# LSH attention and a spatial-gating feed-forward: query heads handled in pairs, on row and column tiles of TensorE

## The chip, the cores and the metric

The kernel runs on one core of a Trainium2 chip. A core has five engines that run their own instruction streams and meet at semaphores: TensorE (PE, matmuls, with its weight loads listed apart as PEld), VectorE (DVE), ScalarE (ACT), GpSimd (POOL) and SyncE (SP), which here only issues DMAs. Matmuls write PSUM; everything else lives in SBUF or in HBM. Sixteen DMA engines move data between HBM and SBUF and inside SBUF, and also transpose 16-bit tiles on the way. The metric is the device time of one execution in microseconds (us), the median of several runs.

## The reference

Inputs are q, k, v of shape 4 batches x 8 heads x 768 tokens x 64, a 64 x 6 hash projection, and the weights of one gated feed-forward. Everything is computed to float32 accuracy.

```python
q_bits = (einsum('bhsd,dk->bhsk', q, proj) > 0); k_bits = (einsum('bhsd,dk->bhsk', k, proj) > 0)
mask = q_bucket[:, :, :, None] == k_bucket[:, :, None, :]      # same 6-bit hash
scores = where(mask, (1 / sqrt(64)) * q @ k.T, -1e9)
scores = scores - max(scores, axis=-1)
attn = exp(scores); attn = attn / (sum(attn, axis=-1) + 1e-9)
x = (attn @ v)                    # heads side by side: batch x 768 x 512
h = maximum(x @ w_in, 0); u, g = h[..., :512], h[..., 512:]
g = (g - mean(g)) / sqrt(var(g) + 1e-6)                        # over the 512
out = (u * (w_spatial @ g + b_spatial[:, None])) @ w_out
```

A query row that matches no key has all scores at -1e9, so its softmax is uniform and its result is the mean of v. The weights w_in and w_out come as float64.

## The kernel before

**Accuracy.** Each float32 operand of a product is carried as two float16 parts, hi and lo, of the operand times a power of two. A product is three float16 products (hi hi, hi lo, lo hi) summed in float32 in PSUM.

**Attention, per head n and block i.** A head has six blocks of 128 rows. There are 32 heads (`N`) in 16 pairs; the two heads of a pair share one load of q and k (`load_qk`), one hash (`hash_rows`), one split (`split_qk`), with head 0 on partitions 0 to 63 and head 1 on 64 to 127. `build` then copies, by DMA, a head's parts into a buffer `ab` of four slots, so that one contraction over 128 rows does two of the three products (q lo with k hi stacked on q hi with k lo), and a second one does q hi with k hi and, on rows 64 to 75, the hash: rows of plus and minus 16384 and 32768 whose products cancel for equal bits and push a score down by multiples of 2^29 for unequal ones.

`scores` makes 128 query rows x 768 keys in two banks of PSUM (four matmuls of 384 columns), takes the row maximum by a VectorE pass whose main output `jk` is thrown away (L287), the exp on ScalarE with that maximum as bias (L289), a float16 hi part by a ScalarE cast (L292), the lo part by a subtraction on VectorE or GpSimd (L293), and a DMA transpose of both parts from `pp` into `pt` (L295), issued from SP's queue. `weighted` sums over keys with the transposed probabilities as stationary operand and v as moving operand, 65 columns wide: the 65th column of ones makes the softmax's sum. `normalize` divides by it, replaces rows without any match by the mean of v (`mean_v`), and writes hi and lo parts of x; `transpose_x` transposes these by DMA for the feed-forward.

Heads 1 to 8 (`KEYS`) go another way, that avoids the transposes: `row_max` computes all hi hi scores once more to get the maxima ahead, writes these as one more row of `ab`, and `scores_k` makes the scores with keys on partitions, so that exp needs no bias and `weighted_k` no transpose.

**Feed-forward, per batch.** `mlp_units` makes 28 units: six v units (x times the second half of w_in, then the normalisation), and per half of the tokens four u units, four s units (spatial product) and three o units (output). In each of these a group of 12 or 18 matmuls fills one bank of PSUM, and ScalarE, VectorE and GpSimd work on its result. The units of a batch are queued when its last head is normalised and then spread over the steps of the next batch by a credit counter. The last batch's units run at the end.

**Order of work.** The program is written as a loop over steps g, one per head and block. Each piece is given a priority by `at(step, k)`, smaller first; a planner simulates the engines and orders each engine's instructions by readiness and priority, one at a time, and semaphores are derived from that order. Engines execute their order strictly. `tc.issue_after(st["tr"])` keeps a DMA behind the latest transpose in SP's queue. Buffers are counted by `bufs`: PSUM has two score tiles of two banks (`ps_sc`), two banks for weighted sums (`ps_pv`) and two for everything else (`ps_m`); in SBUF there are three `ex`, three `pp`, five `pt`. The weights are loaded, converted and split in 37 pieces (`weights_gen`), spread by `W_AT` over the first steps.

Of the kernel before, what the change touches and what calls it, by code (L numbers as in the profile page):

```python
# [10 lines left out]
BF16 = mybir.dt.bfloat16  # L11
# [4 lines left out]
ALU = mybir.AluOpType  # L16
AX = mybir.AxisListType
ET = mybir.EngineType
# [3 lines left out]
NB = 6           # hash bits  # L22
EPS_LN = 1e-6

# Every float32 operand of a product is carried as hi + lo, two float16 parts of
# the operand times a power of two; three products (hh, hl, lh) are summed in
# float32 PSUM.
SQ = 32.0        # q, k, v
SX = 64.0        # x, w_in, gated, w_out
SN = 256.0       # v_n  # L30
SW = 4096.0      # w_spatial
HQ = 16384.0     # hash rows, q side
HK = 32768.0     # hash rows, k side (their product is the mask's penalty)
# [3 lines left out]
def lsh_attention_spatial_gating(  # L37
    ctx: ExitStack,
    tc: tile.TileContext,
    kq: bass.AP,      # [B, NPAIR, 128 = (head, d), (k, q), S]  # L40
    v: bass.AP,       # [B, NPAIR, 128 = p, (c, head), d], token = c * 128 + p
    hconst: bass.AP,  # [128, 34]: proj's columns for each hash row, what a row subtracts, its factor
    w_in: bass.AP,    # [512, 1024]
    w_sp: bass.AP,    # [s, t]
    b_sp: bass.AP,    # [768]
    w_out: bass.AP,   # [512, 512]
    out: bass.AP,     # [B, S, 512]
# [24 lines left out]
    nc.scalar.preload_act_table_set("natural_log_exp_and_others")  # L72
    ident = const.tile([P, P], F16, name="ident")
    make_identity(nc, ident)
    ones = const.tile([P, P], F32, name="ones")
    nc.gpsimd.memset(ones, 1.0)
# [3 lines left out]
    # operands of the scores, per head: slot 0 = q [lo; hi], 1 = k [hi; lo],  # L80
    # 2 = k hi + hash rows + a constant row, 3 = q hi + hash rows + the row of -max
    NAB = 4
    NR = D + 2 * NB
    ab = [const.tile([P, 4, S], F16, name=f"ab{i}") for i in range(NAB)]
    for i, t in enumerate(ab):
        eng = nc.vector if i % 2 else nc.gpsimd
        eng.memset(t[D:P, 2:4, :], 0.0)
        eng.memset(t[96:P, 2, :], HK)
    vp = [const.tile([P, 2 * NT, 130], F16, name=f"vp{i}") for i in range(2)]
    for t in vp:  # L90
        nc.gpsimd.memset(t[:, :, 2 * D:130], 1.0)

# [62 lines left out]
    def load(p):  # L155
        load_qk(p)
        load_v(p)
# [447 lines left out]
```

## Time and profile before

| what | before |
|---|---|
| timed runs, median (3) | 740.17 us (738.73 to 740.52) |
| profiled execution, first to last instruction | span 734.0 us |
| between that span and the timed median | 6.1 us |
| busy, PE / DVE / ACT / POOL | 609.5 / 558.3 / 463.8 / 374.8 us |
| mean granted TensorE clock | 0.940 |
| DMA transposes pt<-pp | 144 |
| operand copies ab<-hl | 65 |

The page names no other time of the profiled execution than its span; the time around it is taken as the difference to the median. In rows of groups, "L293 DVE ... x112 | 118.3, 1057" means line 293, VectorE, 112 instructions, 118.3 us busy in all and 1057 ns listed for one. Instructions on one engine can overlap at their edges, so busy times are less than count times mean, and PE's ends are modelled. In rows of stretches the engines stand in the order PE, PEld, DVE, ACT, POOL, followed by the granted clock (1.00 is full), the DMA share and GB/s. In rows of the time line the first number is the start and the second the length, both in us. In rows of one line, three numbers give the shortest, median and longest in ns. SPq and ACTq are the instruction queues that issue DMAs.

### The profile page before, as it was taken

The numbers are of one execution on the slowest core, as the hardware profiler recorded it, in microseconds if no ns is written. First come the engines' busy times: TensorE is split into PE (matmuls) and PEld (weight loads), VectorE is DVE, ScalarE is ACT, GpSimd is POOL, SyncE is SP. The second block draws the span as 40 slices with busy tenths as digits, with TensorE's granted clock in tenths as the row PEclk, the third lists the DMA queues.
The fourth block names the chain that finished last, engine by engine and source line by source line (L and its number), as shares of the span: only waits on it lengthen the run. The fifth ranks groups of instructions, "written<-read, shape, count | busy, mean of one in ns | idle before, by whom it ended". The sixth has DMA issues, their size and how long they took to land.

```text
span 734.0 us, 15600 instructions
## 1 busy us (share of the span) xinstructions
PE 609.5 (83%) x6024; PEld 365.5 (50%) x6024; DVE 558.3 (76%) x1012; ACT 463.8 (63%) x713; POOL 374.8 (51%) x353
## 2 busy tenths in 40 slices
PE   1686576786796986889898899989998998999997
PEld 0253343444554553555455555555455655654553
DVE  3879989998788899778589888789698876745100
ACT  1565476667878766866677767667677666743221
POOL 4236666669847577457315473436235562541503
PEclk9778888799999898999999999999999999999999
DMA  6783424233299988999999999999999999850011
GB/s 197 177 184 106 122 81 137 77 99 77 57 219 229 226 191 155 237 222 183 231 212 205 188 207 194 221 208 203 220 207 180 205 159 219 171 134 14 1 43 44
DMA packets 274842, 118.24 MB, mean 161 GB/s; under 512 B 255184, under 2 KB 258256, under 8 KB 274768
## 3 DMA queue, kind: packets, MB, share of 16 engines
q1 hardware_dynamic: 272464, 116.36, 76.3%
q10 hardware_dynamic: 2304, 0.89, 0.5%
q8 instruction: 47, 0.77, 0.4%
q14 instruction: 27, 0.22, 0.1%
HBM read 27.94 MB, written 6.29 MB: 47 GB/s over the span
## 4 chain that ended last, share of the span: by engine, by line
PE 33%; DMA 26%; DVE 18%; POOL 7%; issue 7%; ACT 6%; SPq 2%; ACTq 0%; DVEq 0%; POOLq 0%
DMA pt<-pp 21%; PE ups L396 6%; PE ops L426 6%; PE vps L355 5%; PE sps L411 4%; DVE jk L287 2%; DVE mh L229 2%; PE sp L285 2%; DMA ab<-hl 2%; PE sp L286 2%; ACT pp L292 2%; ACT ex L289 2%; PE pv L308 2%; DVE w L137 2%; DVE pp L256 1%
## 5 line engine op out<-in xcount | busy, mean ns | idle before, releaser
L289 ACT ACTIVATE ex<-sp,nb 128x768 f32<-128x768 f32 x144 | 129.1, 898 | 41.5 <-DVE jk L287 35.2
L292 ACT CAST pp<-ex 128x768 f16<-128x768 f32 x144 | 119.1, 829 | 54.9 <-DMA pt<-pp 49.3
L293 DVE TENSOR_TENSOR pp<-ex,pp 128x768 f16<-128x768 f32 x112 | 118.3, 1057 | 42.0 <-ACT pp L292 40.5
L287 DVE TENSOR_SCALAR_CACHE_REDUCE jk<-sp 128x768 bf16<-128x768 f32 x144 | 136.5, 948 | 16.4 <-PE sp L286 12.4
L308 PE MATMUL pv<-vp,pt 128*128 128x65 f16 x864 | 103.4, 197 | 25.7 <-DMA pt<-pp 25.1
L285 PE MATMUL sp<-ab 128*128 128x384 f16 x288 | 96.9, 337 | 32.9 <-ACT ex L289 24.7
L308 PEld LDWEIGHTS <-pt 128*128 128x128 f16 x864 | 82.9, 100 | 49.2 <-DMA pt<-pp 38.8
L310 PE MATMUL pv<-vp,pt 128*128 128x65 f16 x864 | 103.8, 198 | 0.0
L309 PE MATMUL pv<-vp,pt 128*128 128x64 f16 x864 | 103.5, 196 | 0.0
L411 PE MATMUL sps<-ws,vn 128*128 128x384 f16 x576 | 100.3, 327 | 0.0
L286 PE MATMUL sp<-ab 127*128 127x384 f16 x288 | 98.0, 341 | 0.0
L293 POOL TENSOR_TENSOR pp<-ex,pp 128x768 f16<-128x768 f32 x32 | 54.2, 1694 | 82.4 <-ACT pp L292 72.3
L309 PEld LDWEIGHTS <-pt 128*128 128x128 f16 x864 | 82.9, 100 | 11.9 <-issue 1.7
L310 PEld LDWEIGHTS <-pt 128*128 128x128 f16 x864 | 82.9, 100 | 3.4 <-issue 0.6
L396 PE MATMUL ups<-xt,wi 128*128 128x384 f16 x384 | 71.6, 342 | 0.7 <-DVE sg L168 0.7
L411 PEld LDWEIGHTS <-vn 128*128 128x128 f16 x576 | 54.8, 98 | 35.0 <-issue 1.1
L256 POOL TENSOR_TENSOR pp<-ex,pp 128x768 f16<-128x768 f32 x32 | 56.8, 1778 | 30.2 <-ACT pp L255 28.3
L426 PE MATMUL ops<-wo,g 128*128 128x512 f16 x288 | 68.4, 382 | 3.0 <-ACT wo L139 1.1
L355 PE MATMUL vps<-wi,xt 128*128 128x512 f16 x288 | 67.0, 382 | 0.0
L327 POOL TENSOR_TENSOR x<-x,xf 128x384 f32<-128x384 f32 x32 | 37.5, 1171 | 50.7 <-DVE x L326 43.0
L229 DVE TENSOR_REDUCE mh<-mp 128x1 f32<-128x384 f32 x96 | 50.6, 549 | 10.6 <-PE mp L227 9.8
L416 POOL TENSOR_TENSOR sy<-sy,u 128x384 f32<-128x384 f32 x32 | 36.0, 1124 | 44.0 <-DVE sy L415 43.5
(93 smaller groups left out, 1281.4 us busy)
## 6 DMA issues: line engine op xcount, KB each, us to landing
qk<-kq SPq DMA_DIRECT2D x16, 768.0 KB
ab<-hl SPq DMA_DIRECT2D x31, 384.0 KB
ab<-hl SPq DMA_DIRECT2D x34, 192.0 KB
v<-v SPq DMA_DIRECT2D x16, 384.0 KB
out<-o SPq DMA_DIRECT2D x24, 256.0 KB
raw<-w_in SPq DMA_DIRECT2D x16, 256.0 KB
pt<-pp SPq DMA_TRANSPOSE x144
raw<-w_sp SPq DMA_DIRECT2D x12, 192.0 KB
```

Source lines behind the costliest of these rows:

```text
L285: nc.tensor.matmul(ps[:, c], lhsT=t[:, 0, qs], rhs=t[:, 1, cs], start=True, stop=False)
L286: nc.tensor.matmul(ps[:, c], lhsT=t[0:P - 1, 3, qs], rhs=t[0:P - 1, 2, cs], start=False, stop=True)
L287: nc.vector.tensor_scalar(jk, ps, -ISQ, None, op0=ALU.mult, op1=ALU.min, accum_out=nb)
L289: st["ex", n, i] = nc.scalar.activation(ex, ps, AF.Exp, bias=nb, scale=ISQ).ins
L292: nc.scalar.copy(pp[:, 0], ex)
L293: (nc.gpsimd if i in (PL_POOL if n >= 2 * NH else PL_POOL1) else nc.vector).tensor_tensor(out=pp[:, 1], in0=ex, in1=pp[:, 0], op=ALU.subtract)
L308: nc.tensor.matmul(acc, lhsT=pt[:, c, :], rhs=vh, start=(i == 0 and c == 0), stop=False)
L309: nc.tensor.matmul(acc[:, 0:D], lhsT=pt[:, c, :], rhs=vl, start=False, stop=False)
L310: nc.tensor.matmul(acc, lhsT=pt[:, NT + c, :], rhs=vh, start=False, stop=(i == NT - 1 and c == NT - 1))
L396: nc.tensor.matmul(ps[:, :HS], lhsT=wi[gw][:, c, d * P:(d + 1) * P], rhs=xt[c][:, gx, hs], start=(k == 0), stop=(k == 3 * NPAIR - 1))
L411: nc.tensor.matmul(ps[:, :HS], lhsT=vn[gv][:, c, d * P:(d + 1) * P], rhs=ws[gw][:, c, hs], start=(k == 0), stop=(k == 3 * NT - 1))
L426: nc.tensor.matmul(ps, lhsT=gt[h][gg][:, c, j * P:(j + 1) * P], rhs=wo[gw][:, c, :], start=(k == 0), stop=(k == 3 * NF - 1))
```

## The change

The step becomes one pair of heads and one block of 128 queries: 96 steps of two heads each, all on one path. `ab`, `build`, `mean_v`, `row_max`, `scores_k`, `weighted_k`, `normalize` and `transpose_x` are gone, and so are the DMA issues from ScalarE's queue.

- Scores read the split q and k where they lie. Head 0's operands are on partitions 0 to 63, head 1's on 64 to 127; each product is a contraction over 64 rows at `tile_position` (0, 0) or (64, 0) of the array. Four such products per head and half of the keys (lo hi, hi lo, hi hi, and one for the hash rows, which lie in their own buffers `hr`), so 16 matmuls of 384 columns a step, the heads alternating.
- The hash rows are scaled on GpSimd (before: VectorE) and copied to `hr` by eight DMAs per pair from SP's queue.
- The maximum pass clips the scores at -2^27 and writes them to `ex` in SBUF; a row without any match is then flat and needs no special case. GpSimd negates and scales the two maxima, ScalarE takes the exp in place and sums it, GpSimd and a VectorE reciprocal turn the sums into factors, and the cast and the low part apply the factor. So the probabilities are normalised before they are cast. All low parts are on VectorE.
- The transposes write three blocks side by side (`pt` holds half of the queries). `weighted` then takes v as stationary operand, 64 columns for each head at `tile_position` (0, 0) or (0, 64), and the transposed probabilities as moving operand, 384 columns; the result is x already transposed, with both heads below each other, and its two parts are written by one ScalarE and one VectorE operation.
- Steps, buffers and due points follow: 96 steps, `LAG` 2, four `ex`, three `pp`, four (larger) `pt`, two `hl`, and half the values in `W_PTS`.

```diff
+    NHR = 3
+    NR = 2 * NB
+    hr = [const.tile([P, 2, S], F16, name=f"hr{i}") for i in range(NHR)]
...
-        nc.vector.tensor_scalar(s1, s0, hv[:, 1:2], None, op0=ALU.mult)
-        st["sg", p] = s1
+        nc.gpsimd.tensor_scalar(s1, s0, hv[:, 1:2], None, op0=ALU.mult)
+        for e in range(2):
+            for j in range(4):
+                nc.sync.dma_start(
+                    out=hr[p % NHR][D * e:D * e + NR, 1 - j // 2, (j % 2) * HS:(j % 2 + 1) * HS],
+                    in_=s1[32 * j + 16 * e:32 * j + 16 * e + NR, :])
...
+    def scores(p, i):
+        hl, hs = st["hl", p], hr[p % NHR]
+        qs = slice(i * P, (i + 1) * P)
+        ps = [ps_sc.tile([P, 2, 512], F32, tag="sc", name=f"sp{p}_{i}_{e}")[:, :, :HS] for e in range(2)]
         for c in range(2):
             cs = slice(c * HS, (c + 1) * HS)
+            for k, (a, b) in enumerate(((QL, KH), (QH, KL), (QH, KH), (None, None))):
+                for e in range(2):
+                    r = slice(D * e, D * e + D)
+                    lhsT, rhs = (hs[r, 1, qs], hs[r, 0, cs]) if a is None else (hl[r, a, qs], hl[r, b, cs])
+                    nc.tensor.matmul(ps[e][:, c], lhsT=lhsT, rhs=rhs, start=(k == 0), stop=(k == 3), tile_position=(D * e, 0))
...
+        for e in range(2):
+            nc.vector.tensor_scalar(ex[e], ps[e], -float(2 ** 27), None, op0=ALU.max, op1=ALU.max, accum_out=mx[:, e:e + 1])
+        nc.gpsimd.tensor_scalar(nb, mx, -ISQ, None, op0=ALU.mult)
+        for e in range(2):
+            nc.scalar.activation(ex[e], ex[e], AF.Exp, bias=nb[:, e:e + 1], scale=ISQ, accum_out=sm[:, e:e + 1])
+        nc.gpsimd.tensor_scalar(ri, sm, 1e-9, 1.0 / SP, op0=ALU.add, op1=ALU.mult)
+        nc.vector.reciprocal(ri, ri)
+        at(NT * p + i + G_H, 50)
+        h, j = divmod(i, NT // 2)
+        for e in range(2):
+            if j == 0:
+                st["pt", p, h, e] = wk.tile([P, 2 * NT, NT // 2, P], F16, tag="pt", bufs=PTB, name=f"pt{p}_{h}_{e}")
+            pp = wk.tile([P, 2, 2, HS], F16, tag="pp", bufs=PB, name=f"pp{p}_{i}_{e}")
+            nc.scalar.activation(pp[:, 0], ex[e], AF.Copy, scale=ri[:, e:e + 1])
+            nc.vector.scalar_tensor_tensor(out=pp[:, 1], in0=ex[e], scalar=ri[:, e:e + 1], in1=pp[:, 0], op0=ALU.mult, op1=ALU.subtract)
+            st["tr"] = nc.sync.dma_start_transpose(out=st["pt", p, h, e][:, :, j, :], in_=pp.rearrange("p g c k -> p (g c k)")).ins
+
+    def weighted(p, h):
+        vp = st["vp", p]
+        pt = [st.pop(("pt", p, h, e)) for e in range(2)]
+        ps = ps_pv.tile([P, 512], F32, tag="pv", name=f"pv{p}_{h}")[:, :HS]
         for c in range(NT):
+            for k, (gv, gp) in enumerate(((1, 0), (0, 0), (1, 1))):
+                for e in range(2):
+                    nc.tensor.matmul(ps[D * e:D * e + D], lhsT=vp[:, 2 * c + e, gv * D:gv * D + D],
+                                     rhs=pt[e][:, gp * NT + c], start=(c == 0 and k == 0),
+                                     stop=(c == NT - 1 and k == 2), tile_position=(0, D * e))
...
+        x = st["xt", p][:, :, h * HS:(h + 1) * HS]
+        f = SX / (SP * SQ)
+        nc.scalar.activation(x[:, 0], ps, AF.Copy, scale=f)
+        nc.vector.scalar_tensor_tensor(out=x[:, 1], in0=ps, scalar=f, in1=x[:, 0], op0=ALU.mult, op1=ALU.subtract)
...
+    for g in range(NP * NT + LAG + 1):
+        p, i = divmod(g, NT)
+        if p < NP:
+            at(g, 0)
+            scores(p, i)
+            at(g + 1, 300)
+            with tc.issue_after(st["tr"]):
+                if g == 0:
+                    split_v(0)
+                if i == 1 and p + 1 < NP:
+                    hash_rows(p + 1)
+                if i == 2 and p + 1 < NP:
+                    split_qk(p + 1)
...
+        while wv < 2 * NP and 3 * wv + 2 + LAG <= g:
+            m, h = divmod(wv, 2)
+            wv += 1
+            at(g, 200)
+            weighted(m, h)
+            if h == 1 and m % NPAIR == NPAIR - 1:
+                queue += mlp_units(m // NPAIR)
```

284 lines of the change are left out of this document (33 added, 251 removed).

## The prediction

> **What bounds the kernel now.** I read the page first, then the groups by line, then busy time by stretches, then the time line of a few microseconds, and last the chain of waits. A "unit" below is one head's 128 query rows against 768 keys; there are 192, two to a step of the changed kernel, so 96 steps.
>
> ```profile
> span 734.0 us, 15600 instructions
> PE 609.5 (83%) x6024; PEld 365.5 (50%) x6024; DVE 558.3 (76%) x1012; ACT 463.8 (63%) x713; POOL 374.8 (51%) x353
> ```
>
> No engine is full over the span. By stretches, with the busy time of PE, PEld, DVE, ACT, POOL, the granted clock, the DMA share and GB/s:
>
> ```profile
> 20.00:200.00 180.00, 124.57 (x1351) 75.56 (x1350) 159.47 (x287) 119.24 (x191) 112.57 (x103) 0.85 0.44 113
> 200.00:300.00 100.00, 82.79 (x790) 49.33 (x788) 91.84 (x168) 74.69 (x129) 64.08 (x59) 0.90 1.02 202
> 300.00:640.00 340.00, 308.06 (x3284) 190.54 (x3283) 272.26 (x495) 237.90 (x341) 156.59 (x145) 0.98 1.06 205
> ```
>
> and the exps of the third stretch, by line:
>
> ```profile
> L289 ACT ACTIVATE ex<-sp,nb x107: 883/900/923, 299.6 to 638.8; 128x768 f32<-128x768 f32 x107
> ```
>
> Up to 300 us VectorE is the fullest (159/180 = 0.89, then 0.92). From 300 to 640 TensorE is (308/340 = 0.91), while the DMA engines are full. That stretch holds 107 units, 6.36 us per two. The last 75 us are the last batch's feed-forward on TensorE (its rows come below). So DVE early, PE late, and a PE tail must be priced; a DMA saving counts only through waits in the third stretch.
>
> **VectorE, per step.**
>
> ```profile
> 27.25 0.08 DVE L287 DVE_READ_ACCUMULATOR jk<-sp 128x1 f32 x1
> 27.25 0.95 DVE L293 TENSOR_TENSOR pp<-ex,pp 128x768 f16<-128x768 f32 x1
> 28.12 0.95 DVE L287 TENSOR_SCALAR_CACHE_REDUCE jk<-sp 128x768 bf16<-128x768 f32 x1
> ```
>
> ```profile
> L323 DVE RECIPROCAL rv<-rv 128x6 f32<-128x6 f32 x32 | 5.9, 185 | 0.5
> ```
>
> Starts are 0.87 us apart, though each pass is listed with 0.95, and the read of the accumulator starts with the next pass: 0.87 is the price of a 768-wide pass in a full queue. The change gives every unit one max pass and one low-part pass, all on VectorE, and every step one reciprocal: 4 x 0.87 + 0.19 = 3.7 us. The max pass now writes float32 to SBUF; the accumulating pass above wrote bf16, and with float32 in and out from PSUM a plain pass is no dearer (below, L415: 551 ns for 384). I keep 0.87; the upper end is 1.06, the mean listed for L293 on VectorE beside a busy POOL (next fence), which would add 4 x 0.19 x 96 = 73 us of VectorE time. I stay low because POOL loses its 64 low parts and all of normalize.
>
> ```profile
> L293 DVE TENSOR_TENSOR pp<-ex,pp 128x768 f16<-128x768 f32 x112 | 118.3, 1057 | 42.0 <-ACT pp L292 40.5 <-POOL x L327 0.6 <-issue 0.2
> ...
> L177 DVE SCALAR_TENSOR_TENSOR hl<-qk,hl 128x768 f16<-128x768 f32 x16 | 19.2, 1203 | 9.0 <-ACT hl L176 8.7
> ...
> L415 DVE SCALAR_TENSOR_TENSOR sy<-sps,bt 128x384 f32<-128x384 f32 x32 | 17.6, 551 | 40.8 <-PE sps L411 40.6
> L205 DVE SCALAR_TENSOR_TENSOR vp<-v,vp 128x768 f16<-128x768 f32 x16 | 17.5, 1092 | 1.6 <-ACT vp L204 1.6
> L137 DVE SCALAR_TENSOR_TENSOR w<-raw,w 128x256 uint32<-128x256 uint32 x24 | 16.7, 694 | 0.1
> ```
>
> Kept beside it: the splits (two q/k passes of 19.2 become one of double width, v's is 17.5) plus 32 new x low parts at L415's 0.55 (17.6), with the hash thresholds some 80 us or 0.85 a step; four weight passes, the longest 16.7, some 60 us over the first 37 steps, 1.6 each; the feed-forward's L415, bn_stats and the scaling pass, which I take for 60 to 70, 0.7 a step from step 24. That makes 6.15 us for steps 0 to 23, 6.9 for 24 to 36, 5.3 after. Gone are the row-max reductions, normalize and one hash pass. In all 355 + 215 = 570: **VectorE is not relieved**, it only changes its work.
>
> **TensorE, per step.** Starts of matmuls tell the pace, not their listed length.
>
> ```profile
> 501.35 0.33 PE L286 MATMUL sp<-ab 127*128 127x384 f16 x1
> 501.51 0.19 PE L308 MATMUL pv<-vp,pt 128*128 128x65 f16 x1
> 501.54 0.19 PE L309 MATMUL pv<-vp,pt 128*128 128x64 f16 x1
> ```
>
> ```profile
> 659.09 15.54 PE vps L355 x72
> ...
> 728.12 2.39 issue
> ```
>
> From the start of the 384-wide matmul to the next is 0.16 (I use 0.165), from a 65-wide one 0.03. Two units now take 8 x 0.165 + 36 x 0.03 = 2.4 us. After, scores are 16 matmuls of 384 (K = 64, two row tiles), and the weighted sum 36 of 384 per three steps (M = 64, two column tiles): 2.64 + 1.98 = 4.6 us if nothing overlaps, 1.32 + 1.0 = 2.3 if every pair does. So **the tiling, if it works, buys back what it spends**; the saving is 96 row-max matmuls, 16 us, and the v means. Feed-forward stays at 69 us a batch (659.09 to 728.12), 2.9 a step from step 24; hashes add 0.23.
>
> ```profile
> 108.78 0.25 PE L270 MATMUL pv<-vp,pp 128*128 128x65 f16 x1
> 108.95 1.51 PE L163 MATMUL hp<-qk,hc 128*32 128x384 f32 x8
> ```
>
> ```profile
> L163 PE MATMUL hp<-qk,hc x4: 817/849/849, 5.6 to 5.7; 128*32 128x384 f32 x4
> ```
>
> Column tiles do overlap here: the hash's first four start within 0.1 us and each runs 0.82 to 0.85. I take 1.0 for the weighted sum. Row tiles are in no trace. Bounds are 1.32 and 2.64; I take **1.65**, nearer the paired end by the hash row, but not on it: head 0's PSUM tile is freed one pass (0.88) before head 1's, and matmuls are placed singly as they become ready, so part of head 0's run without a partner. The time line shows that habit, a single feed-forward matmul amid pv's:
>
> ```profile
> 508.36 0.19 PE L310 MATMUL pv<-vp,pt 128*128 128x65 f16 x1
> 508.40 0.38 PE L426 MATMUL ops<-wo,g 128*128 128x512 f16 x1
> ```
>
> Going from pv to the hash's tiles took 0.17 between starts where 0.06 was usual: 0.1 a switch, three a step, 0.3 (bounds 0 and, by a whole 0.33 matmul each, 1.0). Late steps: 1.65 + 1.0 + 2.9 + 0.23 + 0.3 = 6.1.
>
> The Trainium skill (TensorEngine Tiling (Array Packing), Key Properties) says that changing the tiling mode drains the array. The hash row agrees that a switch costs something; if a drain were the 0.33 - 0.165 left of one matmul, an estimate, three would be 0.5 and 72 late steps 14 us longer.
>
> **What lies beside.**
>
> ```profile
> L292 ACT CAST pp<-ex 128x768 f16<-128x768 f32 x144 | 119.1, 829 | 54.9 <-DMA pt<-pp 49.3 <-issue 2.2 <-ACT ex L289 1.4
> ```
>
> ```profile
> L318 POOL TENSOR_SCALAR fl<-nb x32: 225/232/1009, 36.2 to 644.0; 128x6 f32<-128x6 f32 x32
> ```
>
> ScalarE has two exps (0.90 in the row of the third stretch) and two casts (0.83) a step, the casts now with a scale per row (0.83 to 0.90, as the exp with its bias), and two sums read out, an operation no row shows: 0 to 0.2, I take VectorE's 0.08. That is 3.7, and with splits, weights and feed-forward (it was busy 463.8, of which exps and casts of 192 units are some 330) about 5.1, under the others; it also sheds 96 DMA issues. POOL's two small operations a step (0.23 each, 1.0 when something is ahead) sit in the chain max, negate, exp, reciprocal, cast; two steps of exp buffers hide them, and without that cover a step would be 7 us of pure chain.
>
> ```profile
> ab<-hl SPq DMA_DIRECT2D x31, 384.0 KB
> ab<-hl SPq DMA_DIRECT2D x34, 192.0 KB
> ```
>
> ```profile
> L295 SPq DMA_TRANSPOSE pt<-pp x144: 1273/1650/4222, 27.2 to 648.1; - x144
> L189 SPq DMA_DIRECT2D ab<-sg x32: 713/714/1280, 12.8 to 118.3; - x32
> ```
>
> ```profile
> 27.21 4.72 DMA pt<-pp
> 510.11 5.94 DMA pt<-pp
> ```
>
> Transposes go from 144 + 16 of x to 192, each 384 KB; 65 copies of 18 MB vanish: nearly the same bytes, spread over the whole run. SP issues 192 x 1.65 + 128 hash copies x 0.71 + some 50 = 458 us, 4.8 a step. All hash copies now stand in SP's queue with the transposes: a burst of 8 x 0.71 = 5.7 us a pair, behind which the next step's two transposes wait, and casts behind them (three pp buffers, each held 0.83 + 0.95 + 4.7 to 5.9 us or more). I cost it at nothing beyond the fill below, as two steps pass before sums are due.
>
> **The sum.** The lead: the hash matmuls start at 5.6 and in two rounds of 0.8 end at 7.2, threshold and scale on idle engines I take for 1.2, then as before from the hash copies to the first max:
>
> ```profile
> 12.76 6.22 SPq L189 DMA_DIRECT2D ab<-sg  x8
> ...
> 21.89 0.95 DVE L287 TENSOR_SCALAR_CACHE_REDUCE jk<-sp 128x768 bf16<-128x768 f32 x1
> ```
>
> 8.4 + 9.1 = 17.5. Steps 0 to 23: 6.15 / 0.94 = 6.55, the fill being between the first stretch's 0.89 and a full queue; 24 to 36: 6.9 / 0.94 = 7.3; the other 59, TensorE: 6.1 / 0.91 = 6.7. That is 157 + 95 + 395 = 647, less one step, as the tail starts with the last: 641. Tail: last step's chain 2 x 0.87 + 0.23 + 2 x 0.9 + 0.23 + 0.19 + 0.83 + 2 x 0.95 and hand-overs, 7.3; two transposes 6.3; 36 sums in pairs 3.0; x 1.1; feed-forward to the end 734.0 - 659.1 = 75: in all 92.7. Span 17.5 + 641 + 92.7 = 751. The profiled execution has 734.0 of span, the timed runs a median of 740.2, so 6.1 lies around it: **757 us**, slower by 2%.
>
> **Rivals.** (1) *Faster, 712.* Row tiles pair fully and the emptier DMA queue lets the engines fill. For it: column tiles overlap, and in the third stretch the DMA share is 1.06, and it should fall. Against: PSUM tiles come free unevenly. Late 5.8 / 0.95 = 6.1, early 6.3, mid 7.0: 602 - 6 + 17.5 + 92.7 + 6.1 = 712. It decides if scores take under 1.4 a step.
>
> The Trainium skill (TensorE: Matmul & The Clock Gate, Part 3) has matmuls on different row tiles start some 4 ns apart and four tiles run 3.07 times as fast; by that rule it is this rival. No run here shows row tiles yet.
>
> (2) *Scores do not pair, 827.* Each head's eight go one after the other: late and mid 7.1 / 0.91 = 7.8, 157 + 72 x 7.8 - 7.8 + 116.3 = 827. (3) *The hash burst stalls SP, 802*: half of 5.7 us lost for 15 pairs, 45 on top of the forecast. (4) *Neither tiling overlaps*, so the change does not do what it says: 8.1 / 0.91 = 8.9, 905.
>
> **Chances.** Forecast 0.40 (its own range 738 to 778), faster 0.33, scores unpaired 0.14, burst 0.08, no overlap 0.05. A difference under 0.3% is what a measurement of this kernel can't tell from none. Faster by more than that: 0.33 and the lowest tenth of the forecast, 0.37; within it 0.07; slower 0.56. For 8 in 10 I leave out the lower part of the faster case and the upper part of 827 with 905: 706 to 832.
>
> **What would show it.** VectorE busy 550 to 590 and above 0.9 until step 37; scores 1.3 (rival 1), 1.65 or 2.6 (rival 2) between a step's first and last start; both heads' weighted matmuls starting together; SP's queue free of multi-microsecond gaps at hash copies; a last stretch of PE near 90 us after the last max. I am wrong if VectorE stays under 0.85 early, or a wait none of these names, on POOL's small operations or on pp buffers, heads the list.

## The result and the profile after

The changed kernel takes 821.7 us (median, 816.5 to 823.0) beside 739.4 us for the kernel before on the same chip: a ratio of 1.113, with a 95% interval of 1.107 to 1.118. It is slower by some 82 us, where the forecast had 17.

The page of the changed kernel, its first lines, the granted clock and the DMA queue:

```profile
span 814.7 us, 12388 instructions
...
PE 709.6 (87%) x4352; PEld 344.7 (42%) x4352; DVE 537.8 (66%) x985; ACT 505.2 (62%) x889; POOL 218.0 (27%) x338
...
PEclk9996675759998876999999999999999899899999
...
q1 hardware_dynamic: 317664, 110.94, 67.0%
```

Busy time by stretches of the same kernel, in the first three the stretches that were shown of the kernel before (PE, PEld, DVE, ACT, POOL, then clock, DMA share, GB/s):

```profile
20.00:200.00 180.00, 144.15 (x750) 65.81 (x748) 136.44 (x266) 124.58 (x223) 36.45 (x73) 0.74 0.81 162
200.00:300.00 100.00, 89.44 (x564) 43.76 (x563) 83.06 (x151) 75.53 (x143) 43.02 (x57) 0.92 0.76 165
300.00:640.00 340.00, 309.97 (x2031) 151.04 (x2029) 234.37 (x420) 219.12 (x379) 87.83 (x139) 0.95 0.71 140
```

From 300 to 640 us TensorE is listed busy for 0.91 of the time, as before the change, but it gets through fewer steps. VectorE, at 0.89 before, stands at 136/180 = 0.76 in the first stretch and at 0.69 in the third, and the DMA share is down from 1.06 to 0.71. In the third stretch no engine has become fuller; in the first, TensorE has, 144/180 = 0.80 in place of 125/180 = 0.69. The groups by line (busy, mean ns, idle before them):

```profile
L186 PE MATMUL sp<-hl 64*128 64x384 f16 x1152 | 238.9, 369 | 39.9 <-DVE ex L194 38.0
...
L207 DVE SCALAR_TENSOR_TENSOR pp<-ex,ri,pp 128x768 f16<-128x768 f32 x192 | 202.3, 1073 | 54.3 <-ACT pp L206 52.8
L206 ACT ACTIVATE pp<-ex,ri 128x768 f16<-128x768 f32 x192 | 172.4, 928 | 46.2 <-DMA pt<-pp 23.2
L194 DVE TENSOR_SCALAR_CACHE_REDUCE ex<-sp 128x768 f32<-128x768 f32 x192 | 180.0, 950 | 19.1 <-PE sp L186 18.1
...
L197 ACT ACTIVATION_READ_ACCUMULATOR ex<-ex,nb 128x1 f32 x192 | 35.9, 187 | 0.0
```

The passes cost close to what was forecast. From start to start in a full queue the max pass takes 0.88 us and the low part 0.94, where 0.87 was taken for both; they are listed with 0.95 and 1.07. ScalarE's reading of a sum is listed with 0.19, but the next instruction starts 0.09 after it, where 0.08 was taken. The waits, where times and longest follow the total:

```profile
ACT ex L197 <- POOL nb L195: 115.6, 58, 6.6
DVE ri L199 <- POOL ri L198: 88.1, 65, 2.9
DVE pp L207 <- ACT pp L206: 52.8, 66, 2.2
PE sp L186 <- DVE ex L194: 38.0, 31, 4.3
ACT hl L166 <- DMA qk<-kq: 30.5, 13, 5.3
```

Before, the longest wait in ScalarE's queue was 49 us. Now the exp stands 116 us for the negated maximum, and VectorE's reciprocal 88 us for the scaled sum. Both hand-overs go through GpSimd.

The first and last start of the max passes give the lead, the length of all steps, and the tail:

```profile
L194 DVE TENSOR_SCALAR_CACHE_REDUCE ex<-sp x192: 919/951/959, 17.0 to 735.4; 128x768 f32<-128x768 f32 x192
```

The last row is head 1's pass; head 0's starts at 734.5. From start to start of head 0's passes, steps 1 to 23 take 6.8 us each, steps 24 to 36 7.9, and the late ones, 37 to 95, 7.8:

| term | forecast | measured | share of the miss |
|---|---|---|---|
| lead | 17.5 | 17.0 | -0.5 |
| steps 0 to 23, each | 6.55 | 6.8 | +6 |
| steps 24 to 36, each | 7.3 | 7.9 | +8 |
| steps 37 to 95, each | 6.7 | 7.8 | **+65** |
| tail from the last step's first max pass | 92.7 | 80.2 | -12 |
| span | 751 | 814.7 | +64 (rounded terms) |

The miss is in the late steps. What TensorE did in them is read from the starts of its matmuls: a 384-wide one counts up to 0.165 us, a 512-wide one 0.216, and what lies beyond is a gap. A late step has 2.0 us of scores, 1.07 of weighted sums, 3.1 of feed-forward and 0.1 of hash, 6.3 in all or 0.80 of the step. The other 1.5 us are gaps: some 0.8 in which a semaphore was awaited, most for transposes and max passes, and some 0.7 without a wait. Of these, the 3.7 changes of tiling in a step take 0.3, about 0.1 each, and most of the rest lies in stretches where the granted clock is halved (it is 0.50 from 296 to 316 us, for one).

Both tilings do overlap. In the time line of the changed kernel (start, length) the weighted sums, and behind them a step's scores with all pairs together:

```profile
516.61 3.11 PE L218 MATMUL pv<-pt,vp 128*64 128x384 f16 x35
...
519.65 0.66 PE L186 MATMUL sp<-hl 64*128 64x384 f16 x6
...
520.15 0.33 PE L186 MATMUL sp<-hr 64*128 64x384 f16 x2
...
520.31 0.65 PE L186 MATMUL sp<-hl 64*128 64x384 f16 x6
...
520.80 0.33 PE L186 MATMUL sp<-hr 64*128 64x384 f16 x2
```

Six score matmuls start within 0.50 us, 0.083 each, half of the 0.165 of one alone, and the 35 weighted ones take 0.089 each. In other steps head 0's tile comes free first and its matmuls go alone. Early on they do so at half pace, as the same kernel's time line shows at 105 us (in brackets the idle time before):

```profile
105.05 1.12 PE L186 MATMUL sp<-hl 64*128 64x384 f16 x3 [4.02 <-DVE ex L194]
...
105.97 0.52 PE L186 MATMUL sp<-hr 64*128 64x384 f16 x1
...
106.29 1.16 PE L186 MATMUL sp<-hl 64*128 64x384 f16 x3
...
107.25 0.52 PE L186 MATMUL sp<-hr 64*128 64x384 f16 x1
```

After 4 us of standing, one head's matmuls start 0.31 us apart (three from 105.05 to 105.97); the granted clock is 0.67 from 100 to 110 us and 0.74 over the first stretch, where the kernel before had 0.85. The Trainium skill (TensorE: Matmul & The Clock Gate, Part 1) puts the cold start-to-start interval at the column count over 1.2 GHz, which makes an estimate of 0.32 us for 384, and says that gaps of some 3.4 us bring it back. These rows agree with both.

### The profile page after: what moved, and what is told of

It reads as the page before. It is cut to its first block, busy times and chain, and to the rows that moved or that the text cites. A ratio compares the mean times of both kernels' runs of the same rounds, so it can differ in the third digit from the quotient of the medians.

```text
span 814.7 us, 12388 instructions
## 1 busy us (share of the span) xinstructions
PE 709.6 (87%) x4352; PEld 344.7 (42%) x4352; DVE 537.8 (66%) x985; ACT 505.2 (62%) x889; POOL 218.0 (27%) x338
## 5 line engine op out<-in xcount | busy, mean ns | idle before, releaser
L186 PE MATMUL sp<-hl 64*128 64x384 f16 x1152 | 238.9, 369 | 39.9 <-DVE ex L194 38.0
L197 ACT ACTIVATE ex<-ex,nb 128x768 f32<-128x768 f32 x192 | 177.4, 925 | 115.9 <-POOL nb L195 115.6
L207 DVE SCALAR_TENSOR_TENSOR pp<-ex,ri,pp 128x768 f16<-128x768 f32 x192 | 202.3, 1073 | 54.3 <-ACT pp L206 52.8
L206 ACT ACTIVATE pp<-ex,ri 128x768 f16<-128x768 f32 x192 | 172.4, 928 | 46.2 <-DMA pt<-pp 23.2
L194 DVE TENSOR_SCALAR_CACHE_REDUCE ex<-sp 128x768 f32<-128x768 f32 x192 | 180.0, 950 | 19.1 <-PE sp L186 18.1
L186 PEld LDWEIGHTS <-hl 64*128 64x128 f16 x1152 | 89.8, 102 | 158.7 <-issue 120.4
L218 PE MATMUL pv<-pt,vp 128*64 128x384 f16 x1152 | 127.4, 361 | 27.5 <-DMA pt<-pp 27.4
L186 PE MATMUL sp<-hr 64*128 64x384 f16 x384 | 120.8, 370 | 1.7 <-DMA hr<-sg 1.7
L195 POOL TENSOR_SCALAR nb<-mx 128x2 f32<-128x2 f32 x96 | 43.6, 454 | 251.5 <-DVE ex L194 241.0
L218 PEld LDWEIGHTS <-vp 128*64 128x64 f16 x1152 | 73.4, 120 | 77.3 <-issue 29.9
```

The source lines that it names most:

```text
L186: nc.tensor.matmul(ps[e][:, c], lhsT=lhsT, rhs=rhs, start=(k == 0), stop=(k == 3), tile_position=(D * e, 0))
L194: nc.vector.tensor_scalar(ex[e], ps[e], -float(2 ** 27), None, op0=ALU.max, op1=ALU.max, accum_out=mx[:, e:e + 1])
L195: nc.gpsimd.tensor_scalar(nb, mx, -ISQ, None, op0=ALU.mult)
L197: nc.scalar.activation(ex[e], ex[e], AF.Exp, bias=nb[:, e:e + 1], scale=ISQ, accum_out=sm[:, e:e + 1])
L206: nc.scalar.activation(pp[:, 0], ex[e], AF.Copy, scale=ri[:, e:e + 1])
L207: nc.vector.scalar_tensor_tensor(out=pp[:, 1], in0=ex[e], scalar=ri[:, e:e + 1], in1=pp[:, 0], op0=ALU.mult, op1=ALU.subtract)
```

## The experiments

Each kernel is the changed one with the edit shown. The changed kernel's own figures are the first row: the ratio to the kernel before on the same chip, the start of the last step's first max pass, and the mean late step, all of the profiled execution but the first two. Ratios of two edits are different where their intervals do not meet. The runs were made on several chips, on which the kernel before took 737 to 741 us; gains in us are taken between medians here, and by the ratios they can differ by some 5 us (no hash copies 17 in place of 12, no loads 27 in place of 23).

| kernel | median us | ratio (95%) | last max at | late step |
|---|---|---|---|---|
| changed kernel | 821.7 | 1.113 (1.107 to 1.118) | 734.5 | 7.8 |
| three score tiles | 887.8 | 1.198 (1.190 to 1.206) | 736.1 | 8.0 |
| one tile for both heads | 886.6 | 1.198 (1.194 to 1.203) | 803.9 | 8.1 |
| heads one after the other | 828.7 | 1.122 (1.116 to 1.127) | 732.7 | 7.7 |
| no factor | 805.0 | 1.089 (1.085 to 1.093) | 709.0 | 7.4 |
| factors per head | 814.9 | 1.105 (1.101 to 1.110) | 721.0 | 7.6 |
| small operations on VectorE | 821.8 | 1.114 (1.109 to 1.119) | 724.2 | 7.4 |
| no hash copies | 809.5 | 1.090 (1.085 to 1.096) | 710.3 | 7.4 |
| no q and k loads | 798.7 | 1.076 (1.070 to 1.081) | 708.2 | 7.5 |
| neither | 801.2 | 1.079 (1.072 to 1.085) | 703.7 | 7.4 |
| hash copies from GpSimd | 834.1 | 1.122 (1.113 to 1.131) | 748.1 | 7.7 |
| third of the feed-forward | 735.9 | 0.997 (0.994 to 0.999) | 680.0 | 6.9 |
| one low part | 809.6 | 1.095 (1.090 to 1.099) | 714.7 | 7.6 |
| three banks for the rest | 829.4 | 1.124 (1.119 to 1.129) | 745.8 | 7.8 |
| six ex buffers | 816.5 | 1.106 (1.100 to 1.112) | 713.7 | 7.6 |
| low parts first | 819.7 | 1.109 (1.104 to 1.113) | 723.7 | 7.6 |
| low parts later | 826.8 | 1.119 (1.115 to 1.124) | 736.5 | 7.8 |
| four pp buffers | 827.3 | 1.117 (1.113 to 1.122) | 735.4 | 7.8 |
| third, and four pp | 718.0 | 0.970 (0.966 to 0.973) | 664.2 | 6.6 |

One thing holds for the whole table. The third batch's feed-forward is spread over the last batch's steps. Where these get shorter, part of it stays over for the tail: in the changed kernel no matmul of the third batch comes after the last score, without the factor 54 do. So a last max that comes 25 us earlier can be worth 17 us in the end. In most of the kernels 28 to 72 matmuls are left over in this way (132 with three score tiles), and at 0.165 to 0.216 us each that alone takes 0.1 to 0.2 us out of a late step, so the medians weigh more than the last column.

### Do score tiles or unpaired scores hold the steps?

Three score tiles, one bank each for the weighted sums and the rest:

```diff
-    PSB = (2,2,2)
+    PSB = (3,1,1)
```

> PSUM is dealt out as three score tiles, one bank for weighted sums and one for the rest (changed kernel: 2, 2, 2). Theory A (the loop scores, two max passes, scores through a single pair of score tiles sets the late step of 7.8 us): head 0 of the next step can be computed during the max passes, the late step falls to about 6.9 and the time from 822 to 760, less what the single other banks cost. Theory B (TensorE is overloaded by scores that do not pair, 1.98 us a step in place of 1.32): no gain, 815 to 850. Theory C (the chain of small operations through GpSimd, max to cast): no gain, 815 to 830.

One score tile of four banks for both heads, so that every pair of matmuls is ready together:

```diff
-        ps = [ps_sc.tile([P, 2, 512], F32, tag="sc", name=...)[:, :, :HS] for e in range(2)]
+        both = ps_sc.tile([P, 4, 512], F32, tag="sc", name=...)
+        ps = [both[:, 2 * e:2 * e + 2, :HS] for e in range(2)]
...
-    PSB = (2,2,2)
+    PSB = (1,2,2)
```

> The two heads' scores of a step share one four-bank tile, so all 16 matmuls come free together and stay in their alternating order; same PSUM. Theory B: scores go from 1.98 to 1.35 us a step, the late step loses 0.6 to 0.7, 822 to about 775. Theory A: head 0 can no longer start one pass earlier, the loop stays as long, 810 to 850. Theory C: no change, 815 to 830.

Head 0's eight matmuls, then head 1's:

```diff
-        for c in range(2):
-            for k, (a, b) in enumerate(...):
-                for e in range(2):
+        for e in range(2):
+            for c in range(2):
+                for k, (a, b) in enumerate(...):
```

> The score matmuls are written head 0 first, then head 1, so row tiles can only overlap by accident. Theory B: scores cost 2.64 us a step, 0.66 more, 822 to about 880. Theory A: head 0's maximum can start after 1.3 us and overlaps head 1's matmuls, the loop is not longer, 800 to 830. Theory C: 815 to 830.

Measured: 888, 887 and 829 us. With three tiles the steps end at the same time (last max at 736.1 in place of 734.5) and the loss is in the tail, 140 us, where the feed-forward has a single bank. So a third tile buys nothing that can be seen here, although the bank taken from the feed-forward may hide a gain in the late steps. In steps 1 to 23, where no feed-forward needs that bank, a step takes 6.75 us in place of 6.82. With one tile, its time line (start, length) shows every pair together, as in the good step above:

```profile
509.88 0.66 PE L187 MATMUL sp<-hl 64*128 64x384 f16 x6
...
510.38 0.33 PE L187 MATMUL sp<-hr 64*128 64x384 f16 x2
...
510.54 0.65 PE L187 MATMUL sp<-hl 64*128 64x384 f16 x6
...
511.03 0.33 PE L187 MATMUL sp<-hr 64*128 64x384 f16 x2
```

Scores take 1.32 us a step, the lower bound, yet steps are 8.1 to 8.6 us, as scores and max passes now wait for each other. Row tiles pair as well as can be. Conversely, without any alternation scores take 2.4 us of a late step in place of 2.0, and the median is 7 us higher, within the intervals. **So 0.4 us more of unpaired scores a step cost nothing that can be told from none.** What full pairing would be worth with two tiles no run shows, as the shared tile brings a wait of its own.

### Do the hand-overs through GpSimd hold them?

No factor: this kernel leaves out the division by the softmax's sum.

```diff
-        nc.gpsimd.tensor_scalar(ri, sm, 1e-9, 1.0 / SP, op0=ALU.add, op1=ALU.mult)
-        nc.vector.reciprocal(ri, ri)
...
-            nc.scalar.activation(pp[:, 0], ex[e], AF.Copy, scale=ri[:, e:e + 1])
-            nc.vector.scalar_tensor_tensor(out=pp[:, 1], in0=ex[e], scalar=ri[:, e:e + 1], in1=pp[:, 0], op0=ALU.mult, op1=ALU.subtract)
+            nc.scalar.activation(pp[:, 0], ex[e], AF.Copy)
+            nc.vector.tensor_tensor(out=pp[:, 1], in0=ex[e], in1=pp[:, 0], op=ALU.subtract)
```

> The division by the softmax's sum is left out (no factor, no reciprocal; cast and low part take the exp as it is), so the result lacks the normalisation. Theory C: the chain from exp to cast loses two hand-overs and two small operations, some 1.3 us a step, 822 to 720-760. Theories A and B: these steps lie beside the loop or TensorE, 800 to 822.

Negation and factor per head, so that neither head waits for the other:

```diff
-        nc.gpsimd.tensor_scalar(nb, mx, -ISQ, None, op0=ALU.mult)
+            nc.gpsimd.tensor_scalar(nb[:, e:e + 1], mx[:, e:e + 1], -ISQ, None, op0=ALU.mult)
...
-        nc.gpsimd.tensor_scalar(ri, sm, 1e-9, 1.0 / SP, op0=ALU.add, op1=ALU.mult)
-        nc.vector.reciprocal(ri, ri)
+        for e in range(2):
+            nc.gpsimd.tensor_scalar(ri[:, e:e + 1], sm[:, e:e + 1], 1e-9, 1.0 / SP, op0=ALU.add, op1=ALU.mult)
+            nc.vector.reciprocal(ri[:, e:e + 1], ri[:, e:e + 1])
```

> Each head has its own negation of the maximum and its own factor (GpSimd operations 2 x 2 a step in place of 2, reciprocals 2 in place of 1), so head 0 goes on without waiting for head 1. Theory chain: head 0's exp starts one pass (0.9 to 1.7 us) earlier and its cast one exp earlier; steps shorten by 0.8 or more, time 720 to 770. Theory TensorE: late steps stay at 7.8, 96 x 0.19 more VectorE in the early steps, time 815 to 835.

Both small operations on VectorE:

```diff
-        nc.gpsimd.tensor_scalar(nb, mx, ...)
+        nc.vector.tensor_scalar(nb, mx, ...)
...
-        nc.gpsimd.tensor_scalar(ri, sm, ...)
+        nc.vector.tensor_scalar(ri, sm, ...)
```

> The negation of the maximum and the sum's scaling move from GpSimd to VectorE, so four hand-overs between engines a step become two and no step waits for GpSimd. Theory chain: the waits of exp for the negation (115.6 us over the run) and of the reciprocal for the sum's scaling (88.1) shrink by what the two hand-overs and GpSimd's own time are, 2 x (0.25 + 0.3) = 1.1 us a step at most: time 750 to 800. Theory TensorE: late steps stay, and VectorE pays 2 x 0.1 to 0.2 us in every early step: 820 to 835.

Measured: 805, 815 and 822 us. With the small operations on VectorE the two great waits of the list have other names in the list of waits and most of their length (total, times, longest):

```profile
ACT ex L197 <- DVE nb L195: 93.9, 50, 6.4
...
DVE ri L198 <- ACT ex L197: 61.2, 58, 2.9
```

So GpSimd was only the last in the row: the exp waits for what stands ahead of the negation, not for GpSimd. The late steps do fall to 7.4 us, 23 us in all, of which an estimated 10 are the 50 matmuls left over for the tail; but the early steps take 7.2 in place of 6.8 and the tail 96 in place of 80, and the median does not move. The theory of the chain had promised 20 to 100 us here, and falls as the main cause. Taking the factor out whole is worth 17 us.

### Do the loads and the hash copies in SP's queue?

No hash copies from the fourth pair on (older hash rows are used again), no loads of q and k after the second pair (the second pair's are used again), and both:

```diff
-        for e in range(2):
+        for e in range(2 if p < NHR else 0):
...
+        if p > 1:
+            st["qk", p] = st["qk", p - 1]
+            return
```

> The eight copies of hash rows per pair are left out from the fourth pair on (its scores then use old hash rows, so the mask is wrong). Theory D (each pair, SP waits for the scaled hash rows and issues eight copies, some 10 us in which no transpose is issued, and the three pp buffers run dry): the steps at block 1 and block 5 fall from 10.5 and 8.5 us to the others' 6.5 to 7.5, about 5 us a pair or 70 us in all, 822 to about 750. Theory C (small operations): 805 to 822. Theory B (unpaired scores): 815 to 822.

> q and k are loaded for the first two pairs alone and the later pairs use the second's (their results are wrong). Theory E (the split waits on ScalarE's queue for the load of q and k, 30 us of idle time in 13 waits, because the one buffer is loaded late and behind transposes): 822 to about 785. Theory D: 805 to 822, the copies stay.

> Both are left out. If D and E both hold and add: 822 to about 715 to 725, late steps 6.5 us. If something else sets the steps: above 780.

The hash copies issued from GpSimd's queue:

```diff
-                nc.sync.dma_start(
+                nc.gpsimd.dma_start(
```

> The eight hash copies a pair are issued by GpSimd in place of SP; nothing is left out. Theory D: SP is free for the transposes, 822 to about 755 to 770, unless GpSimd's own issue of eight copies delays the two small operations that stand between maximum and exp. Without D: 815 to 830.

Measured: 809, 799, 801 and 834 us. The burst in SP's queue is there, as the time line of the changed kernel shows (start, length):

```profile
438.77 0.86 SPq L142 DMA_DIRECT2D v<-v  x1
...
441.03 1.25 POOL L155 TENSOR_SCALAR sg<-sg,hc 128x384 f16<-128x384 f16 x1
...
442.31 6.10 SPq L158 DMA_DIRECT2D hr<-sg  x8
...
448.52 1.47 SPq L208 DMA_TRANSPOSE pt<-pp  x1
```

No transpose is issued from 438.7 to 448.5. That is the longest of fifteen such stretches, which take 6.7 to 9.8 us, 7.7 in the mean. But without these copies only 12 us are gained, without the loads 23, without both 20: the gains do not add. From GpSimd's queue the copies free nothing: the median is 12 us higher (7 by the ratios), the intervals just overlapping.

### Does an engine's load?

A third of the feed-forward: this kernel leaves out the products hi lo and lo hi there (the ends of the groups, `stop`, follow).

```diff
-    THREE = ((0, 0), (0, 1), (1, 0))
+    THREE = ((0, 0),)
```

> Leaves out two of the three products (hi lo and lo hi) of every feed-forward matmul group; all the work of the other engines, the number of units and their buffers stay. In the late steps TensorE then has 2.0 + 1.1 + 2.9 / 3 + 0.2 = 4.3 us a step in place of 6.2; the tail loses up to two thirds of its 69 us. Theory TensorE (the late steps are set by TensorE's own work, as the forecast had it, only at a fill of 0.80): late steps fall from 7.8 to about the 5.3 / 0.85 = 6.2 us that VectorE leaves, and time to 820 - 59 x 1.6 - 40 = 685. Theory chain (late steps are set by how max, negate, exp, sum, reciprocal, cast and low part of two heads follow each other over three engines): late steps stay above 7.2, and only the tail gains: 740 to 785.

One low part: head 1's low part of the probabilities is left out (zeros, written by GpSimd).

```diff
+            if e:
+                nc.gpsimd.memset(pp[:, 1], 0.0)
+            else:
                 nc.vector.scalar_tensor_tensor(out=pp[:, 1], in0=ex[e], ...)
```

> Leaves out the low part of head 1's probabilities: GpSimd writes zeros there, in place of a VectorE pass. VectorE has 0.9 us less in every step, TensorE the same work. Theory VectorE at 0.85: early steps fall by 0.87 / 0.85 = 1.0 to 5.8, the middle ones alike: 36 us. For the late steps: if both engines add up there (as the 0.9 us that fell from 1.9 us less TensorE work suggest), they fall by about half of 0.9, another 26: 755 to 765. If TensorE alone sets the late steps: 780 to 790. If the hand-overs do, and VectorE's load is of no matter: 805 to 820.

Measured: 736 and 810 us. Busy time by stretches of the kernel with a third of the feed-forward:

```profile
20.00:180.00 160.00, 127.23 (x640) 58.09 (x639) 121.10 (x237) 109.92 (x195) 31.11 (x64) 0.73 0.80 161
280.00:680.00 400.00, 332.17 (x2012) 155.26 (x2010) 309.11 (x555) 288.24 (x500) 128.03 (x188) 0.82 0.79 158
```

and of the kernel with one low part (columns as before):

```profile
20.00:180.00 160.00, 124.35 (x677) 59.59 (x673) 108.06 (x224) 114.83 (x203) 46.32 (x90) 0.79 0.83 167
280.00:680.00 400.00, 353.39 (x2378) 174.47 (x2376) 231.26 (x451) 260.01 (x452) 133.68 (x222) 0.93 0.72 143
```

TensorE loses 1.9 us of a late step and the step 0.9, so neither theory's figure (6.2 us, or above 7.2) was met. Between the two profiled executions lie 75.5 us; 53 of them come from the late steps, 21 from the tail. TensorE's granted clock falls from 0.94 to 0.82 with the lighter load (280 to 680 us), which takes some of the gain back: of the 1.0 us that a late step does not give back, 0.4 are matmuls in stretches of halved clock, counted by starts, and 0.5 are longer waits.

VectorE loses 0.87 us of every step, 83 us in all, and the kernel gains 12: early steps go from 6.8 to 6.6, late ones from 7.8 to 7.6, of which the 60 matmuls left over for the tail make up 0.2. But the pass is not simply gone. GpSimd writes the zeros, 0.74 us a step, and its order is strict too (total, times, longest):

```profile
DVE ri L199 <- POOL ri L198: 133.6, 78, 5.0
...
POOL pp L208 <- DMA pt<-pp: 72.1, 34, 5.4
```

The zeros wait 72 us for a free pp buffer, and VectorE's wait for the scaled sum, which stands in the same queue, grows from 88 to 134 us. **So TensorE's load counts for about half of itself in the late steps. VectorE's pass gave back a seventh of itself in this run**; how much more it would without GpSimd's zeros, no run shows. The theory of VectorE at 0.85 had the early steps at 5.8 in this run, and nothing here speaks for it.

### Do the buffers or the written order?

One bank moved from the weighted sums to the rest:

```diff
-    PSB = (2,2,2)
+    PSB = (2,1,3)
```

> One PSUM bank moves from the weighted sums (2 to 1) to the feed-forward and the hash (2 to 3). Theory TensorE, fill: TensorE stands because a feed-forward group waits for a bank, and with a third bank late steps shorten by 0.3 or more and the tail by up to 10: 780 to 800. Theory chain: late steps keep 7.8, the tail may gain a few us: 810 to 825.

Six ex buffers:

```diff
-    NHR = 3
+    NHR = 2
...
-            v32[i] = wk.tile([P, F2], F32, tag="v32m", bufs=4, ...)
+            v32[i] = wk.tile([P, F2], F32, tag="v32m", bufs=3, ...)
...
-            o = wk.tile([P, DM], F32, tag="v32m", bufs=4, ...)
+            o = wk.tile([P, DM], F32, tag="v32m", bufs=3, ...)
...
-    EB = 4
+    EB = 6
```

> Six ex buffers in place of four, paid for with two hash-row buffers in place of three and three feed-forward result buffers in place of four; the work is the same. Three steps can then be between max pass and low part at once. Theory depth (TensorE with 6.2 and VectorE with 5.9 us a late step stand for each other because only two steps are in flight): late steps come to 7.2 or less, and time to 770 to 795. Theory order (the engines' written orders set the waits, not the number of buffers): 810 to 830.

Low parts first, and (in its place `G_H = 2`) low parts later:

```diff
-    G_H = 1
+    G_H = 0
```

> Casts, low parts and transposes get the priority of their own step in place of the next one's, so in VectorE's order the low parts come ahead of the next step's max passes; the work is the same. Theory order: the max passes and with them the next scores come later, ScalarE waits longer for the negated maxima: 830 to 870. Theory load: within 5 of 821.

> Casts, low parts and transposes get the priority of two steps on, so max passes that are ready come ahead of them, and ScalarE's exps ahead of casts. Theory order: TensorE's score tiles come free earlier, late steps fall towards 7.2: 780 to 800. Theory load: within 5 of 821; since only two pairs of ex exist, the max passes of two steps on can't start before these low parts anyway.

Four pp buffers, alone and with the third of the feed-forward (`THREE` as above; it leaves out the same two products):

```diff
-    NHR = 3
+    NHR = 2
...
-    PB = 3
+    PB = 4
```

> Four pp buffers in place of three (paid for with two hash-row buffers in place of three). In the changed kernel a pp buffer is held 8.7 us in the early steps, from the start of its cast to the landing of its transpose, so two casts a step through three buffers need 2 x 8.7 / 3 = 5.8 us a step at least, and 43 of 100 early casts start within 0.5 us of a landing; in the late steps it is 7.5 us, 5.0 a step, and 19 of 100. Theory pp ring (the ring paces the early steps, TensorE the late ones): early steps fall from 6.8 to 6.2 to 6.4, late ones stay within 0.2 of 7.8, time 800 to 812. Theory neither: within 5 of 821. If late steps too fall below 7.4, the ring was a cause there as well: 785 to 798.

> Leaves out two of the three products of every feed-forward group, as in the run with a third of the feed-forward, and has four pp buffers and two hash-row buffers. In that run the late steps stood at 6.9 us with a pp buffer held 8.3 us (5.5 a step at least) and 45 of 100 late casts starting within 0.5 us of a landing. Theory pp ring: with TensorE's work reduced the ring is the next bound, and a fourth buffer brings early and late steps to 6.2 to 6.5, time 735 - 0.5 x 95 = 690 to 705. Theory VectorE (its 5.9 us a step at 0.86 is the floor of 6.9): late steps stay at 6.8 to 6.9, time 725 to 737.

Measured: 829, 817, 820, 827, 827 and 718 us. Three banks for the rest are just clear of the changed kernel's interval, and slower; the intervals of the next four overlap with it. Neither depth of ex nor the order of max passes against low parts nor the pp ring is a single cause: with four pp buffers early steps take 6.9 us, no less than with three, and each buffer is simply held longer (10.2 us in place of 8.7, from the cast to the landing). With TensorE's load reduced the fourth pp buffer does help: late steps 6.6 in place of 6.9, 718 in place of 736 us. It then had a wait to take away that TensorE had covered.

No version here beats the kernel before with the whole computation done; the two that reach or beat it leave feed-forward products out.

## Why the prediction was right and wrong

**Slower: right, and the time within the range; the size wrong by 65 us.** 822 lies within 706 to 832, but only because the range reaches up towards the rival of unpaired scores; the forecast's own range ended at 778. The lead and the costs of the passes came out as worked.

**Late steps, the term that failed: "6.1 / 0.91 = 6.7", measured 7.8.** Two mistakes in it can be told apart. First, the work: without the switches it was 5.8 us and is 6.3 by the same starts. Scores are 2.0 in place of 1.65 (0.36 too little; the bounds 1.32 and 2.64 held), feed-forward 3.1 in place of 2.9 because units that the middle steps had not done were made up here, hash 0.1 in place of 0.23. Second, the fill: 0.91 was read from listed busy time, 308 of 340 us, while the work was counted by starts, which are closer together than the listed lengths. By starts (0.032 us for a 65-wide one) the kernel before fills 0.86 of that stretch. The listed busy share of the changed kernel is 0.91 too, so that figure came true and said nothing. With 0.86 the forecast would have had 7.1 us, 24 us more in all.

The rest of the gap, 0.86 down to 0.80, is not more waiting: counted by starts, TensorE awaits a semaphore for 0.11 of the time in both kernels (0.7 us of 6.4 before, 0.8 of 7.8 now). New are the gaps without a wait, 0.15 us per two units before and 0.7 a late step now. Nearly half of these are the changes of tiling, 0.3 us, as forecast, which the forecast counted as work; most of the others lie where the clock is halved (granted clock 0.95 from 300 to 640 us, where it was 0.98). With the changes of tiling as work, a late step has 6.6 us in place of 6.1 and a fill of 0.85, close to the 0.86 of before. So the two terms of the fraction account for the miss, some 32 us for the work and as much for the fill. That the fill by starts is about the same in two such different orders of work may be luck; no run shows why.

**What sets the late steps.** TensorE's load, for about half of its weight: shown by the run with a third of the feed-forward. What the other half is stays open. The factor (17 us), the loads (23), the hash copies (12) and one VectorE pass (12) each give a little back, separate heads nothing beyond the intervals, and what is taken from one wait can turn up at the next, as in the run that put the small operations on VectorE. That would fit engines which each run a strict order with few buffers between them: from 300 to 640 us VectorE stands for 0.31 of the time and ScalarE for 0.36, by listed busy time. That picture is only argued; what share the written order has in it was tried by moving one priority, and stays open.

**Early steps: the right number for a wrong reason.** 6.55 was VectorE's 6.15 at 0.94; measured 6.8. But VectorE is listed busy for 0.76 there, under the 0.85 at which the prediction called itself wrong (and for 537.8 us in all, under the 550 to 590 it named), and the run that takes a pass from it changes the step by 0.2. Six ex buffers change it by 0.3, a third score tile, a fourth pp buffer and the loads by 0.1 or less. The rows at 105 us point to TensorE, with unpaired scores at half pace: in steps 1 to 23, 158 of 365 score matmuls begin 0.29 to 0.34 us after their predecessor though nothing is awaited, and TensorE is listed busy for 0.80. No run settled it.

**The small operations of GpSimd: the prediction's other sign of error came true.** They head the list of waits with 116 and 88 us, "two steps of exp buffers hide them" did not hold as written, and yet moving them gained nothing in the median. A long wait in a list is where a chain is cut, not what it costs.

**The tail: 80 for 92.7.** I took the last batch's feed-forward to begin after the last weighted sums. Its first units read only x's first half of the tokens, which is finished three blocks earlier; two of their matmuls start at 727 us and 52 of the other 70 from 732, ahead of the last weighted sums at 746.85 (time line of TensorE, start and length):

```profile
732.01 4.94 PE L242 MATMUL vps<-wi,xt 128*128 128x512 f16 x22
739.13 6.64 PE L242 MATMUL vps<-wi,xt 128*128 128x512 f16 x30 [2.17 <-ACT vr L246]
...
746.85 3.08 PE L218 MATMUL pv<-pt,vp 128*64 128x384 f16 x35 [0.81 <-DMA pt<-pp]
```

**The rivals.** Faster (1) had its condition half right: pairs do reach 1.32 us, and the DMA share fell, but neither filled the engines; the run with every pair together is slower. The Trainium skill's rule that it named (TensorE: Matmul & The Clock Gate, Part 3: matmuls on different row tiles start some 4 ns apart) agrees with the trace: in the rows at 519.65 the two matmuls of a pair start 3 to 4 ns apart, and the next pair 0.16 us later. Unpaired scores (2) gave the nearest time, 827, by luck: scores took 2.0 us, not 2.6, and in the run with the heads one after the other 0.4 us more of them a step cost 7 us, within the intervals. The hash burst (3) exists, 7.7 us without a transpose per pair in the mean, and leaving it out is worth 12 us, where 45 were given. No overlap (4) is out.

## What to carry to other kernels

Count work and fill in the same measure: if matmuls are priced by their starts, the fill must come from starts too, and a change of tiling or a spell of halved clock must stand on the same side of the fraction in both kernels. Read so, the fill was 0.86 before and 0.85 after, where listed busy time gave 0.91 for both. In a step with six hand-overs between engines from max pass to low part, and two steps in flight, taking one wait, buffer or pass away gave back a fraction of its length here. When a pairing on the array depends on two buffers that come free at different times, expect it in part of the steps only, and ask what pairing is worth in the end: giving up what there was of it cost 7 us of 822 here, within the intervals, and forcing it by a shared tile cost 65.

## What the runs showed of the hardware

- Two row tiles of 64 rows, and two column tiles of 64 columns, each run in pairs at 0.083 and 0.089 us a matmul of 384, twice the pace of one; a change of tiling costs about 0.1 us (0.11 in the mean of 43 in the late steps where nothing was awaited).
- TensorE's granted clock follows its load within the same kernel: 0.94 in the late steps, 0.82 with two thirds of the feed-forward's matmuls gone, 0.74 in the early steps, where it stands four times for 3.2 to 4.3 us. These are means of stretches at 1.00 and at 0.50. A lighter TensorE is in part a slower one.
- Reading out a sum is listed with 0.187 us on ScalarE, and the next instruction starts 0.09 after it; VectorE's reading of a maximum is listed with 0.08 and starts with the next pass. Eight copies of 9 KB keep SP's queue for 6.1 us.
